# A new order for the same 887 operations of an attention and squared-ReLU kernel, with PSUM rooms shared between its stages

## The chip, the cores and the metric

The kernel runs on one core of one Trainium2 chip. The metric is the device time of one execution in microseconds (us). Three runs of the kernel before took 212.10, 212.76 and 213.73 us; the median is 212.76.

## The reference

Attention with a sliding window of 128 keys and four sink keys, then a two-layer network with a squared ReLU; cut to what is computed:

```python
# q, k, v: (4, 8, 768, 64); n_sink 4; window 128; w_in: (512, 2048); w_out: (2048, 512); float32
scores = (q @ k.transpose(0, 1, 3, 2)) / sqrt(64)
rel = pos[:, None] - pos[None, :]
keep = (pos[None, :] < n_sink) | ((rel >= 0) & (rel < window))
a = softmax(where(keep, scores, -1e9))
x = (a @ v).transpose(0, 2, 1, 3).reshape(3072, 512)
g = maximum(x @ w_in, 0) ** 2
out = g @ w_out                                   # (3072, 512) float32
```

## The kernel before, in words

**Tiling.** The four batches b = 0 to 3 are worked through one after another, with their stages overlapped. A batch has 768 tokens, in three strips s = 0, 1, 2 of 256. Attention of a strip runs in groups: score matmuls (L607) into PSUM, an exponential on ScalarE (L628) that writes `expm` in bf16, masks on `expm` (`domask`: on VectorE, L637 and L640, or as an affine select on GpSimd, which has line L215), the products with v (`values`, L676), and a norm on VectorE (L692 and L693) that gives `xn`. The four sink keys go by `sink_scores` (L566). For batches 0 and 1 queries and keys are transposed on TensorE (L500), and the result of a strip by a bridge on TensorE (L725); for batches 2 and 3 both are DMA transposes on SP's queue: qkT (L454) and xT (L707).

**Layer 1** of batches 0 and 1 is a plain product (L757) with a relu on ScalarE or VectorE (L768, L770) and a square. For batches 2 and 3, `layer1_fast` replaces eight block products by seven: it works on two units, strip 0 alone and strips 1 and 2 together, each in parts of `quad`. Here unit (2, strip 0) or (2, s0) is the first unit of batch 2, and (2, s1) the second. A unit first needs sums of halves of xT (`total`, `xs`, L845, on VectorE); its part is seven products into one PSUM room (L887), numbered as in `product(name, ...)` and run in the order 1, 2, 5, 4, 3, 6, 7. Product 1 needs the first sum. After product 1 `first` copies a bank to `t` (L189 or L191), `less` subtracts product 2 and product 5 from it (L928, VectorE), the relu on the room (L943) must come between products 4 and 3 and the products 6 and 7 that go into the same room, and a custom instruction on VectorE (L955) adds `t`, takes the relu and frees the room. Squares (L909 on ScalarE, L911 on VectorE) write `gT_sb`.

**Layer 2** works on units (b, u) of 256 tokens, u = 0, 1, 2. Two units of batch 0 are plain (L976). The others are `layer2_fast`, with seven products named c, d, a, b, c, d, a by the quarter of the output that they go into (L1086, 8 matmuls of 256 columns each); sums s1 to s4 of `gT_sb` (L1044) come before, and copies and additions (L189, L191, L1111, L1127 `last_quarter`, L1134 `middle`, `first_quarter`) after, into one of two rooms of `osb`, which a 512 KB store on SP (L1163) empties. The last unit, (3, 2), stores in parts (L1156, L1172, L1175).

**Order.** No scheduler decides at run time. The operations are recorded into a plan (`op(...)`: engines with costs, what they come after, which rooms they take and which they release) and issued in the order of the string `ORDER`: one word for each of the 887 operations, the number of the operation, then a letter where the engine is chosen (d VectorE, a ScalarE, g GpSimd), then `+k` where one of several PSUM pools is chosen:

```python
            o.engine = names[word[-1]] if word[-1] in names else next(iter(o.engines))
            for s in o.takes:
                if len(s.pools) > 1:
                    s.pool = s.pools[int(chosen.pop(0))]
                s.room = free[s.pool].pop(0)
```

Each engine runs its own operations in this order; waits between engines follow from the data and from rooms taken over. PSUM is four rooms of two banks each, in two pools of two:

```python
    sizes = dict(att=2, den=2, qr=5, qs=6, expm=8, r=3, osb=2, sg=4, u=2)
```

`att` serves attention and `den` the layers, apart from the first group of batch 0, the groups of batch 1 and `quad`, which may choose. Loads of q, k and v are casting DMAs on GpSimd's queue (L367, L376, L396, L408), for batch 0 also on SP.

Of the kernel before, what the change touches and what calls it, by code (L numbers as in the profile page):

```python
# [21 lines left out]
0 7 8 9 1 5 10 11 2 12 13 3 14 15 55d 57+0 16 19 59a 20 17 56d 21 18 61d 63+0 22 58 62d 65a 60d 64 6 67a 83+1 79 66a  # L22
68d 69+1 85 70 71d 103+0 84+0 105 73g 74d 72d 23 75+1 86 76 77d 91+0 78a 24 87+1 93 25 89 88 92+0 80 26 114+1 90 94
95+0 4 96 117 97 106g 99+1 98 104+0 107 100d 101 118g 81+1 102d 113+0 108d 156 115 127 27 28 29 30 31 32 33 34 35 36
37 38 116d 82 109+0 111 39 40 41 119+1 121 157a 158a 110 112 120 122 162 123+1 125 163d 168 169d 126a 124a 171 172a
170a 159 160d 177 128 131 165 173d 161d 132d 178d 166d 164a 130a 129a 133a 144 146 136 138 174 145 137 289 290 148
134 175a 140 135 176a 147d 167d 139d 291 179d 292 293 141d 142 143 149g 42 43 44 45 46 150 151 47 48 49 50 51 52 53
54 365 366 367 368 208g 369 370 371 372 373 294 295 152 154 296 153d 155d 297d 298d 186 187d 180 181a 200+0 204+1
192+0 201 193 205 194a 206d 195a 189 207d 182d 203a 196+0 197 183 198a 190a 191a 188d 199d 202d 274 212+0+0 184d 209
278 279 215 213 237+0+0 210+1 211 238 240 185d 300 301 275 214 302 241d 276 277 303 280 281 282 304 219+0+0 283 222  # L30
220 306a 305 307 230+0+0 309a 233 231 308 311 223 216 221 310 239d 224+0 312 234g 232g 299 385 386 384 383 313 225
314 242+0 217+0 243 218 284 315 316 235+0 236 285 251+0 286a 287a 317d 252d 253d 244+0 246 226+1 228 247d 227d 245a
248+1 229a 399 322 249d 250d 402 400 323d 355 401 256+0+0 259 257 340 254+0 255 341a 258d 358 356 342a 396 260d 334
335a 374 375 376 377 378 379 380 381 395g 388 390 387 288 392 391 318 389 393 394 331 263+0+0 332a 261+1 264 266 319
262 267d 324d 406 333a 407 320a 337 409 265g 382 597 268+0 598 599 600 601 602 603 604 605 606 607 608 609 610 338a
321d 403 269 328 627d 410 270+0 272 404 408 329a 271a 273d 359 325 405 339a 336a 326a 346 347d 357 327a 415 418 419d
330d 352 411 353a 416 412 354d 447 448 343 344a 345a 349 422 423 425 417g 426g 611 451 452 397 363 449 453d 350d 398
450 351a 348a 454 455 457 466 456a 438 458 459 441 439 467 485 486 489 490 487 460 488 461 361 492 431 491a 432 434
615 413 616 622 620 619 493 462 494d 468 463 464a 414 465 621 617 618 420 440g 612 424g 427 496 433g 442g 428 498
421 470 471 443 435g 436 472a 504a 495 362 499 497 500 473 444 437 508 505 469 628 501 475d 474 477 647 429 625 445  # L40
430 446 650 502a 648 624 503 623 626 360 476 478 481 507 479 506 480 364 482 483d 523+0 525a 524 631 527 526 528 634
632 509+0 510 529 511d 512 530 531a 654 538 633 539 513 514 515 655 533 534 657 649g 656g 516 517a 638 613 614 535
635 536d 537 641 519 520 532a 636 658g 651g 521 639 569+0 570 637 571a 629 583+0 630 572 573 585a 640 522a 518a 574
584 587 575 576 586 555+1 642 589 577a 588 643 679 557a 540 556 590 559 591a 592a 578a 558 560 579 580 593 594 581
561 562 595 541+0 542 683 563a 564a 543d 545 544 680 546 565 547 566 548 684 686 644 567 685a 596a 549a 582a 681
550d 689 682 645 484 646 670 551 552 687 690 673 671 674g 553 688a 554a 663 691 694 666 664 665g 568d 698 692 693
699 659 652 702 703 705 667g 672g 695 696d 700 653 717 660 718 721 668 697 661 736a 704a 669 737 675 676 701 722 739
740 738 708 677 678 662 755+1 706 709 741+1 742 757a 719 720 756 743a 723a 707d 759 745 724 758 761 725 744 760 762
763a 764a 711 746 727 710 713 726a 765 766 747 712 769 714 771 767 728 730 715d 772 748 749a 729 815+0 816 817a 732
770 731 818 733 819 751 752 787+1 734a 735 716 801+0 802 803a 789a 753 820 804 768d 821 788 822 773+1 805 791 754a  # L50
823a 824a 775a 790 806 750d 792 829 807 774 793 776 825 808 794 826 809a 827 830 831 795a 796a 810a 777 779 811 778
812 797 798 833 780 834 836 813 799 828a 835a 781a 832 838d 839 783 784 782a 800a 814a 837 840 841 844 785 786d 842
848 849 852 853 855 843 845 846d 867 854a 850 851 858 857d 868 871 847 856 859 873a 861 862 860 863 864 869 872 865a
866 870 877 874 876a 875 878 880 881 886 879 882 883 885 884
# [59 lines left out]
def kernel(  # L114
# [267 lines left out]

    def load_natural(b, s, older_values):

        P.group = ("load", b)
        begun = [ops["layer1", b - 2, 0, 0], w_out_op[3]]
        for ti in (1, 0):
            if s == 0:
                qn_slot[b, ti] = Slot("qr", NT)
            for i in range(2):  # L390
                t = 2 * s + i

                def run(e, t=t, ti=ti):
                    if t == 0:
                        qn_t[b, ti] = bank(qn_slot[b, ti], "qn", [128, NT, DM], BF16)
                    return [nc.gpsimd.dma_start(  # L396
                        out=qn_t[b, ti][:, t, :].rearrange("p (h d) -> p h d", d=D),
                        in_=(q, k)[ti][b, :, 128 * t:128 * t + 128, :].rearrange("h p d -> p h d"))]
                o = dma_op("pool", ("qk", b, ti, t), run, 64 * 0.032,
                           None,  # L400
                           [qn_slot[b, ti]] if t == 0 else ())
                o.after += begun
                if b - 1 in FAST:
                    o.after += [ops["wi", 1, 0]]
                o.margin = 1.661
        for t in (2 * s, 2 * s + 1):
            def run(e, t=t):
                return [nc.gpsimd.dma_start(  # L408
                    out=v_sb[b % 2][:, t, :, 0:D],
                    in_=v[b, :, 128 * t:128 * t + 128, :].rearrange("h p d -> p h d"))]  # L410
            o = dma_op("pool", ("v", b, t), run, 64 * 0.032)
            o.after += begun + older_values
            o.margin = 1.661
# [6 lines left out]
    def attention(b, key):  # L420
# [3 lines left out]
        begun = [ops["layer1", b - 1, 0, 0]] if b >= 2 and b not in NATURAL else []  # L424
# [12 lines left out]
        def stage(g, f0, f1, side):  # L437
# [4 lines left out]
            def at(f):  # L442
                return key(f0 + (f1 - f0) * f)
# [94 lines left out]
            if g == 0:  # L538
                def sink_keys(e):
                    for h2 in range(2):  # L540
                        r = slice(64 * h2, 64 * h2 + 64)
                        nc.vector.tensor_copy(
                            out=kb[r, :].rearrange("p (m c) -> p m c", c=136)[:, :, 4 * h2:4 * h2 + NSINK],
                            in_=qkT_sb[r, :, 1, 0, 0:NSINK])
# [11 lines left out]
                A["sink_keys"] = op(at(0.1), {"dve": 0.34}, sink_keys,  # L556
# [189 lines left out]
    def layer1(b, key, fbs, c0, cw, need):  # L746
# [3 lines left out]
        bs, rs = Slot("den", 1), Slot("r", 1)  # L750
# [10 lines left out]
        ops["layer1", b, fbs[0], c0] = a  # L761

# [97 lines left out]
    def quad(b, ss, qd, key, xs, sums, slots, part, landed, whole):  # L860
# [15 lines left out]
        def product(name, bk, n, fresh, after):  # L876
# [19 lines left out]
            ops["layer1", b, (f0, name), ss[0]] = o  # L896
            return o
# [19 lines left out]
        m1 = product(1, 0, 0, True, [o for x, o in ops.items() if x[0] == "layer1" and x[1] == b - 1])  # L917
# [43 lines left out]
    def layer2(b, u, keys, by_part=False):  # L961
        P.group = ("l2", b, u)
        bs = Slot("den", 2)
# [57 lines left out]
    def layer2_fast(b, u, key):  # L1021
# [33 lines left out]
        bs, os_, us = Slot("den", 1 if tail else 2), Slot("osb", 1), Slot("u", 1)  # L1055
        ys = Slot("att", 1) if tail else bs
# [84 lines left out]
        pairs = out[128 * g:128 * g + 256, :].rearrange("(i p) m -> p i m" if b in FAST and u else "(p i) m -> p i m", i=2)  # L1141
# [23 lines left out]
        def store_rest(e):  # L1165
            o = bank_t["osb", b, u]
            if b not in FAST or not u:
# [15 lines left out]
    NATURAL, TURNED, BIASED, FAST = (2, 3), (), 1, (2, 3)  # L1183
# [24 lines left out]
    for b in range(B):  # L1208
        if b == 0:
# [3 lines left out]
            at(1, 0.2, 0.725, "att")  # L1213
# [4 lines left out]
        elif b in FAST:  # L1218
            layer1_fast(b, (0,), lambda i, b=b: b + 0.167 * i / 2, 0.01)
            layer1_fast(b, (1, 2), lambda i, b=b: b + 0.167 + 0.34 * i / 4, 0.01)  # L1220
        else:
            for i, fb in enumerate(range(0, NFB, 2)):
                layer1(b, b + 0.34 * i / 8, (fb, fb + 1), 0, 512, (0, 1))
        for i, fb in enumerate(range(0, NFB, 4) if b not in FAST else ()):
            if b == 0:
                layer1(b, 0.2 + 0.226 * i / 4, range(fb, fb + 4), 512, 256, (2,))
            else:
                layer1(b, b + 0.34 + 0.167 * i / 4, range(fb, fb + 4), 512, 256, (2,))
        if b + 1 == FAST[0]:
            weight_sums_in(b + 0.4, [ops[x] for x in ops if x[0] == "layer1" and x[1] == b])  # L1230
        if b + 1 < B:
# [7 lines left out]
            else:  # L1239
                attention(b + 1, lambda f, b=b: b + LO + (HI - LO) * f)(0, 0.0, 1.0, "att")  # L1240
        if b == 0:
            weight_sums(0.6, [w_out_op[i] for i in range(4)])
        for u in range(NS):
            if b == 0 and u < 2:
# [40 lines left out]
```

## Time and profile before

| | |
|---|---|
| median of three runs | 212.76 us (212.10 to 213.73) |
| span of the profiled execution | 210.2 us |
| median less span | 2.56 us |
| TensorE busy | 201.4 us, 96% |
| TensorE weight loads, beside the matmuls | 169.4 us, 81% |
| VectorE busy | 170.8 us, 81% |
| ScalarE busy | 126.6 us, 60% |
| GpSimd busy, its DMA issues included | 101.8 us, 48% |
| granted TensorE clock | 0.99 to 1.00 |
| end of the last matmul | 206.7 us of 210.2 |

The profile is one execution, and the list of times doesn't say which of the three runs it belongs to; its own time is its span and some 2 to 3.5 us that lie around it. In the profile PE is TensorE, DVE VectorE, ACT ScalarE, POOL GpSimd and SP the queue of SyncE; L943 is line 943 of the kernel. A line of a group or of the timeline names the operation, the tile written and the tiles read. What stands behind an arrow in a line of waits is what ended the wait.

### The profile page before, as it was taken

How to read it: one execution, taken by the hardware profiler on the slowest of the kernel's cores; microseconds unless marked ns; L12 is line 12 of the kernel's file. 1: busy time of each engine (PE TensorE's matmuls, PEld its weight loads, DVE VectorE, ACT ScalarE, POOL GpSimd, SP SyncE). 2: the span in 40 equal slices, each digit the busy share in tenths (PEclk: the TensorE clock that was granted, in tenths of full speed). 3: DMA queues.
4: the chain of work that ended last, by engine and by line, in shares of the span. 5: the costliest groups of instructions: out<-in, count | busy, mean ns of one | idle time of the engine just before them, and what ended most of it. 6: DMA issues, size and time to landing. Idle time of an engine off the chain costs nothing.

```text
span 210.2 us, 5719 instructions
## 1 busy us (share of the span) xinstructions
PE 201.4 (96%) x2383; PEld 169.4 (81%) x2383; DVE 170.8 (81%) x317; ACT 126.6 (60%) x162; POOL 101.8 (48%) x143
## 2 busy tenths in 40 slices
PE   3999999999999999999999999799999999999993
PEld 3859996689468845679789988699899999999892
DVE  7487567366999964789997988999989978999863
ACT  2498287407744579898952268889870244896110
POOL 7999774898877941999369023700253000000000
PEclk9999999999999999999999999999999999999998
DMA  5999999999999999999987639700512300400222
GB/s 171 278 188 206 171 201 214 161 155 205 153 112 157 104 150 252 138 124 144 149 102 151 103 77 179 50 3 0 150 62 69 75 5 38 166 0 0 103 100 100
DMA packets 93881, 26.09 MB, mean 124 GB/s; under 512 B 86816, under 2 KB 91552, under 8 KB 93856
## 3 DMA queue, kind: packets, MB, share of 16 engines
q0 software_dynamic: 69248, 12.59, 81.3%
q1 hardware_dynamic: 24424, 13.07, 27.9%
q8 instruction: 18, 0.29, 0.6%
q10 hardware_dynamic: 184, 0.07, 0.1%
q14 instruction: 7, 0.06, 0.1%
HBM read 27.30 MB, written 6.29 MB: 160 GB/s over the span
## 4 chain that ended last, share of the span: by engine, by line
PE 94%; DVE 2%; ACT 1%; POOL 1%; issue 1%; POOLq 0%; DVEq 0%
PE py L1086 29%; PE pm L757 20%; PE pm L887 17%; PE po L676 7%; PE py L976 7%; PE ps L607 6%; PE pt L500 3%; PE pt L182 2%; PE px L725 1%; ACT expm L628 1%; PE ya L1086 1%; PE ps L600 1%; PE pk L566 1%; DVE r L955 1%; DVE gT_sb L911 0%
## 5 line engine op out<-in xcount | busy, mean ns | idle before, releaser
L215 POOL TENSOR_SCALAR_AFFINE_SELECT expm<-expm 128x512 bf16<-128x512 bf16 x42 | 29.2, 724 | 49.5 <-ACT expm L628 24.5
L628 ACT ACTIVATE expm<-ps 128x1024 bf16<-128x1024 f32 (+1 forms) x48 | 43.8, 950 | 12.4 <-PE ps L607 11.3
L757 PE MATMUL pm<-xT,w_in_sb 128*128 128x256 bf16 (+1 forms) x320 | 44.7, 294 | 0.0
L757 PEld LDWEIGHTS <-w_in_sb 128*128 128x128 bf16 x320 | 34.2, 114 | 6.6 <-issue 0.9
L1086 PEld LDWEIGHTS <-gT_sb 128*128 128x128 bf16 x336 | 31.1, 98 | 4.2 <-issue 0.5
L1086 PEld LDWEIGHTS <-sg 128*128 128x128 bf16 x240 | 22.8, 98 | 3.3 <-issue 0.5
L768 ACT ACTIVATE r<-pm 128x1024 bf16<-128x1024 f32 x14 | 14.3, 1022 | 13.5 <-PE pm L757 13.4
L887 PEld LDWEIGHTS <-w_in_sb 128*128 128x128 bf16 x256 | 21.8, 114 | 0.5 <-issue 0.2
L887 PE MATMUL pm<-xs,wi 128*128 128x128 bf16 (+1 forms) x192 | 19.5, 246 | 1.5 <-DVE xs L845 0.9
L1086 PE MATMUL py<-wt,gT_sb 128*128 128x256 bf16 x160 | 20.8, 273 | 0.0
L1086 PE MATMUL py<-wt,sg 128*128 128x256 bf16 x160 | 20.6, 273 | 0.0
L909 ACT ACTIVATE gT_sb<-r 128x1024 bf16<-128x1024 bf16 x18 | 18.4, 1051 | 0.3
L1086 PE MATMUL py<-w_out_sb,gT_sb 128*128 128x256 bf16 x144 | 18.5, 273 | 0.0
L189 ACT ACTIVATE osb<-py 128x256 f32<-128x256 f32 (+1 forms) x15 | 6.2, 410 | 20.3 <-DMA out_dram<-osb 6.0
L770 DVE TENSOR_SCALAR r<-pm 128x1024 bf16<-128x1024 f32 x10 | 12.2, 1222 | 7.5 <-PE pm L757 4.3
L887 PEld LDWEIGHTS <-wi 128*128 128x128 bf16 x192 | 16.4, 113 | 2.2 <-issue 2.1
L693 DVE TENSOR_TENSOR xn_sb<-po,rc 128x512 bf16<-128x512 f32 (+1 forms) x28 | 17.2, 615 | 1.0
L676 PEld LDWEIGHTS <-expm 128*128 128x128 bf16 x352 | 16.3, 97 | 1.4 <-issue 0.5
L676 PE MATMUL po<-v,expm 128*128 128x65 bf16 x352 | 17.3, 193 | 0.1
L943 ACT ACTIVATE r<-pm 128x1024 bf16<-128x1024 f32 x12 | 12.1, 1021 | 8.1 <-PE pm L887 7.9
L928 DVE TENSOR_TENSOR t<-t,pm 128x512 f32<-128x512 f32 x24 | 15.9, 680 | 0.9 <-ACT t L189 0.4
L955 DVE CUSTOM_DVE_ANT_1 r<-pm,t 128x1024 bf16<-128x1024 f32 x12 | 14.5, 1220 | 1.6 <-PE pm L887 1.5
(97 smaller groups left out, 381.9 us busy)
## 6 DMA issues: line engine op xcount, KB each, us to landing
out_dram<-osb SPq DMA_DIRECT2D x11, 512.0 KB, 4.5
v<-in_v_dram POOLq DMA_DIRECT2D x24, 128.0 KB, 7.1
qn<-in_k_dram POOLq DMA_DIRECT2D x20, 128.0 KB, 7.1
qn<-in_q_dram POOLq DMA_DIRECT2D x20, 128.0 KB, 6.9
w_in_sb<-in_moe_w_in_dram POOLq DMA_DIRECT2D x4, 512.0 KB, 10.2
w_out_sb<-in_moe_w_out_dram POOLq DMA_DIRECT2D x4, 512.0 KB, 10.4
qr<-in_k_dram SPq DMA_DIRECT2D x4, 256.0 KB, 5.1
qr<-in_q_dram SPq DMA_DIRECT2D x4, 256.0 KB, 4.8
```

What stands on the lines that cost most here:

```text
L215: nc.gpsimd.affine_select(out=e_tile, in_=e_tile, compare_op=ALU.is_ge, fill=fill, base=i - 1, pattern=[[0, n], [1 if i else -1, 128]], ch ...
L628: nc.scalar.activation(out=x[:, :, o:512], in_=bank_t["s", b, s, m][:, :, o:512], func=AF.Exp, scale=scale)
L676: touch(("po", b, s, m0), e, nc.tensor.matmul(pv[:, i, h2, :], lhsT=lhsT, rhs=rhs, start=(n_ == 0), stop=(n_ == len(mms) - 1)), j)
L693: touch(("po", b, s, m0), e, nc.vector.tensor_tensor(out=xn_sb[:, 2 * s:2 * s + 2, 128 * (m0 + j0):128 * (m0 + j0 + nj)].rearrange("p i (j ...
L757: nc.tensor.matmul(pm[:, i, :], lhsT=w_in_sb[:, fb // 4, kb, fb % 4:512:4], rhs=xT[:, c0 // 256:(c0 + cw) // 256, kb, :], start=(kb == 0), ...
L768: nc.scalar.activation(out=o, in_=h, func=AF.Relu)
L887: touch(tag, e, nc.tensor.matmul(y[:, bk, i, :], lhsT=weights(name, f0 + i, a), rhs=rhs[:, a, :], start=fresh and i == 0 and a == 0, stop= ...
L909: nc.scalar.activation(out=d, in_=x, func=AF.Square)
L928: touch(tag, e, nc.vector.tensor_tensor(out=T["t"], in0=T["t"], in1=T["y"][:, bk], op=ALU.subtract), bk)
L955: touch(tag, e, nc.vector._custom_dve(TENSOR_ADD_SAT, out=r.rearrange("p b n c -> p b (n c)"), in0=T["y"].rearrange("p b n c -> p b (n c)" ...
L976: touch((b, u), e, nc.tensor.matmul(pm[:, i, :], lhsT=gT_sb[:, fb, 128 * t:128 * t + 128], rhs=w_out_sb[:, fb, :], start=(fb == 0), stop=( ...
L1086: ins = nc.tensor.matmul(y_, lhsT=x[:, i, :], rhs=r_, start=(first or tail and n == 2) and i == 0, stop=i == HB - 1, skip_group_check=not ...
```

## The change

The set of operations stays as it is. What changes is

- the string `ORDER`, from about the 24th operation of TensorE on (18.6 us in the trace of before). 267 operations stand on VectorE in place of 274, 170 on ScalarE in place of 161, 100 on GpSimd in place of 102; TensorE keeps 290 and SP 60. Two of the layer-1 relu, the copies of sink keys and some copies go from VectorE to ScalarE, two squares of `quad` the other way; four masks go from GpSimd to VectorE and three back;
- the pools: layer 1, layer 2 and attention may take rooms of `att` and of `den` alike, as the words say;
- bounds on the order that the recorder set: the first product of a `quad` no longer comes after all of the older batch's layer 1, attention no longer after its first product, and the loads of batches 2 and 3 come after whichever layer-1 product was recorded first;
- the copy of sink keys may run on ScalarE;
- `FAST` becomes a table of units, with the same units in it, and the weight sums are recorded later, which shifts numbers in `ORDER`. The tests `b in FAST` turn into `natural` with the same outcome.

In the order of TensorE the stretch from the last product of layer-2 unit (1, 1) to the first product of unit (2, 0) reads, in its first part (numbers are `quad` products; "8" and "12" matmul score groups are `ps`):

```
before: a(1,1) | 1 2 ps 5 | 1' 2' 4 3 ps 5' 4' 6 7 3' ps | 6' 7' values(3,0) | 1 of (2,s1)
after:  1 d(1,1) a(1,1) 2 ps 5 4 1' values(3,0) 2' 3 5' ps 4' 6 3' sinks(3,0) 7 | 1 of (2,s1) | 6' 7' | 2 of (2,s1)
```

(a dash marks the second part of unit (2, s0)). Of VectorE's operations, two sums `xs` of unit (2, s1), the second of them the one that its product 1 needs, stand directly behind `first_quarter` of unit (1, 1); in before that sum is the third of three, and four `less`, a `first`, two masks, a custom relu and a square stand, beside the other two sums, between `first_quarter` and it.

The code, cut to its core:

```diff
 ORDER = """
-0 7 8 9 1 5 10 11 2 12 13 3 14 15 55d 57+0 16 19 59a 20 17 56d 21 18 61d 63+0 22 58 62d 65a 60d 64 6 67a 83+1 79 66a
...
+0 7 8 9 1 5 10 11 2 12 3 55d 13 57+0 14 56d 15 19 20 16 21 61d 59a 17 22 63+0 18 6 62d 58 79 65a 64 60d 67a 68d 83+1
...
 """
+    first_layer1 = {}
...
-        begun = [ops["layer1", b - 2, 0, 0], w_out_op[3]]
+        begun = [first_layer1[b - 2], w_out_op[3]]
...
-        begun = [ops["layer1", b - 1, 0, 0]] if b >= 2 and b not in NATURAL else []
+        begun = []
...
-                A["sink_keys"] = op(at(0.1), {"dve": 0.34}, sink_keys,
+                A["sink_keys"] = op(at(0.1), {"dve": 0.34, "act": 0.42}, sink_keys,
...
-        bs, rs = Slot("den", 1), Slot("r", 1)
+        bs, rs = Slot(("den", "att"), 1), Slot("r", 1)
...
-        m1 = product(1, 0, 0, True, [o for x, o in ops.items() if x[0] == "layer1" and x[1] == b - 1])
+        m1 = product(1, 0, 0, True, [])
...
-        bs = Slot("den", 2)
+        bs = Slot(("den", "att"), 2)
...
-        bs, os_, us = Slot("den", 1 if tail else 2), Slot("osb", 1), Slot("u", 1)
-        ys = Slot("att", 1) if tail else bs
+        bs, os_, us = Slot(("den", "att"), 1 if tail else 2), Slot("osb", 1), Slot("u", 1)
+        ys = Slot(("att", "den"), 1) if tail else bs
...
-    NATURAL, TURNED, BIASED, FAST = (2, 3), (), 1, (2, 3)
+    NATURAL, TURNED, BIASED = (2, 3), (), 1
+    FAST = {2: ((0,), (1, 2)), 3: ((0,), (1, 2))}
...
-            at(1, 0.2, 0.725, "att")
+            at(1, 0.2, 0.725, ("att", "den"))
...
-                attention(b + 1, lambda f, b=b: b + LO + (HI - LO) * f)(0, 0.0, 1.0, "att")
+                attention(b + 1, lambda f, b=b: b + LO + (HI - LO) * f)(0, 0.0, 1.0, ("att", "den"))
```

## The prediction

> **What bounds the kernel now.** I read the page's busy line and slices first, then the waits of TensorE, then the windows, the chain of waits, and last the timeline of the one place where TensorE stands still.
>
> The page:
>
> ```profile
> PE 201.4 (96%) x2383; PEld 169.4 (81%) x2383; DVE 170.8 (81%) x317; ACT 126.6 (60%) x162; POOL 101.8 (48%) x143
> PE   3999999999999999999999999799999999999993
> DVE  7487567366999964789997988999989978999863
> ```
>
> TensorE works 201.4 of the span's 210.2 us; only the first, the last and one slice in the middle fall below 9. The order in which 290 TensorE operations stand cannot shorten the work in them, so all that a new order of the same operations can win is the time in which TensorE stands. The waits of TensorE:
>
> ```profile
> PE pt L182 <- POOL ident L239: 3.5, 1, 3.5
> PE pm L887 <- DVE xs L845: 0.9, 1, 0.9
> PE pm L887 <- ACT r L943: 0.7, 1, 0.7
> ```
>
> The first is the start: nothing to multiply yet. The other two stand together in the one thin slice. The windows of 10 us around it (columns: stretch, length, busy TensorE, weight loads, VectorE, ScalarE, GpSimd, clock, DMA share, GB/s):
>
> ```profile
> 120.00:130.00 10.00, 10.00 (x153) 8.81 (x152) 8.68 (x19) 6.70 (x9) 1.60 (x3) 1.00 0.77 133
> 130.00:140.00 10.00, 8.46 (x109) 7.60 (x107) 9.78 (x15) 9.01 (x12) 5.49 (x8) 1.00 0.49 41
> 140.00:150.00 10.00, 10.00 (x100) 9.31 (x98) 9.76 (x16) 8.71 (x10) 0.00 (x0) 1.00 0.09 23
> ```
>
> From 130 to 150 VectorE is busy 9.8 of each 10 us: here, and nowhere else for long, it and not TensorE sets the pace. The clock is full. The chain of waits through this place (start, length, what):
>
> ```profile
> 128.13 1.92 PE pm L887 x32
> ...
> 130.18 1.22 DVE r L955
> 131.41 0.61 DVE expm L637
> 132.02 1.04 DVE gT_sb L911
> 133.06 0.78 DVE xs L845
> 133.84 0.04 issue
> 133.88 1.03 PE pm L887 x8
> ```
>
> For 3.65 us the end of the kernel hangs on four VectorE instructions in a row. The last, the sum xs for unit (batch 2, strips 1 and 2), is what TensorE needs; the three ahead of it are nothing to it. Now the timeline of the same place (start, length, engine, line):
>
> ```profile
> 130.53 1.02 ACT L943 ACTIVATE r<-pm 128x1024 bf16<-128x1024 f32 x1
> 131.60 1.05 PE L887 MATMUL pm<-xs,wi 128*128 128x128 bf16 x16 [0.68 <-ACT r L943]
> 131.94 1.12 DVE L911 TENSOR_TENSOR gT_sb<-r 128x1024 bf16<-128x1024 bf16 x1
> 132.57 1.75 POOL L215 TENSOR_SCALAR_AFFINE_SELECT expm<-expm 128x512 bf16<-128x512 bf16 x2
> 132.98 0.85 DVE L845 TENSOR_TENSOR xs<-xT 128x512 bf16<-128x512 bf16 x1
> 133.88 0.49 PE L887 MATMUL pm<-xs,wi 128*128 128x256 bf16 x3 [0.86 <-DVE xs L845]
> ```
>
> TensorE stands 0.68 and 0.86 us by the records; counted against its usual rate per matmul (0.109 us for 256 columns, 16 in 1.75) it loses 0.9 and 1.0 there, and 0.1 to 0.2 more at 134.9 and 137.3: some 2.1 us. Before 17 us there are stalls of 0.4 and 0.3 behind the first exponentials (L628), at the end 3.5 us from the last matmul at 206.7 to 210.2. The profiled span is 210.2 and the median run 212.76, so 2.56 us lie around the span (1.9 to 3.5 by the three runs); the sum below is made on the span, and 2.56 added.
>
> **The change part by part.** The operations are the same 887. Up to about 18 us every queue is the same (TensorE's first 24 operations, VectorE's 22, SP's 12), so start and early stalls stay: 0. The last seven products stand in the same order. Store (3,1) is issued some 1.3 us later on SP, behind VectorE's middle sum; the copies into the output room that wait for store (3,0) now have 7 products of 0.87 = 6.1 us of TensorE as cover, against a 512 KB store's median landing of 4.5 us plus 1.1 for the evacuation: 0, and 0.5 to 1 if a landing is late.
>
> Freer PSUM pools (layer1, layer2 and the attention of batches 1 to 3 may use any of the four rooms) issue nothing and remove no work. TensorE in the profile of before waits nowhere for a room that its readers hold longer than about 0.2 us outside 130 to 138, so what they can win elsewhere is 0, and they make the new order possible. The score groups, which cost TensorE 0.12 us each at their end, have as many neighbours of other kinds as before: 0.
>
> Engine moves over the whole kernel: VectorE 274 to 267 operations, ScalarE 161 to 170, GpSimd 102 to 100. Two relu of 1.22 go from VectorE to ScalarE (1.02), copies and sink keys too, two squares of 0.7 come back. VectorE loses some 2 us of 170.8, but outside 120 to 165 it covers nothing that TensorE waits for: 0 there.
>
> Stall one (0.9). Product 6 of unit (2, strip 0) waits for the relu at 130.53, which ran on a ScalarE that had two exponentials ahead; between the product before and it TensorE had one score group (0.44). In the new order there stand sink scores, a product 7 and a product 1: 0.44 + 0.45 + 0.44 = 1.33, which is 0.89 more, as long as the stall. Gone, unless VectorE or ScalarE come later.
>
> Stall two (1.0). The xs sum that product 1 of the next unit waits for is now the second of two right behind the first-quarter copy of unit (1,1), ahead of all that held it back. That wait is gone, but what VectorE did meanwhile stays to be done. So I compare the whole stretch, from the last product of unit (1,1) to the first layer2 product of (2,0). Before: VectorE 30 instructions, 19.2 us busy; it lasted 20.2, TensorE's own work in it is 18.1. After, 32 instructions by the row means: four r at 1.22, twelve t at 0.68, three xs at 0.49 and one at 0.68, two masks at 0.56, two squares and two sg at 0.75, norms 1.8, copies 1.1: 22.2, less the overlap of 0.06 that the timeline shows where one follows another at once, 31 times, is 20.3. TensorE's work in the new stretch is 19.4, as other products have moved in. VectorE therefore still misses TensorE's pace by 0.9, where TensorE lost 2.1 before. Saved: 1.2. Before, the same sum gives 21.2 - 1.7 = 19.5 and 20.2 was needed: 0.5 of idle time ahead of r at 130.18 and hits above the mean. I leave that 0.7 out after, since the sums stand earlier and three of eight GpSimd selects have left the stretch; with it 0.5 is saved. The bounds are 0 (VectorE's total sets the end, whatever stands first) and 2.1.
>
> The contention with GpSimd is in these rows: xs of 128x512 took 0.42 at 127.86 and 0.85 at 132.98 with a select beside it, the square L911 0.69 and 1.12: about 0.43 for a hit. The instructions that read PSUM (r 1.22, t 0.68) take the same time with and without. The five selects left can cost up to 5 x 0.43 = 2.2, of which the row means hold a part already. The Trainium skill (SBUF — State Buffer, "Who interferes with whom") has the rule: a VectorE instruction with two SBUF inputs and a GpSimd one that reads SBUF exclude each other for the whole instruction, whichever began first. By it a hit could cost as long as a select, 0.72, rather than the 0.43 seen, and VectorE would lose up to 5 x 0.72 = 3.6; it also speaks against any order that merely moves the selects. The trace shows nothing above 0.45, and 0.43 is taken.
>
> What is late next. The early xs sums need all of xT, so the last two transposes on SP (L707). On TensorE 7.1 us stand between the second values group of (2,2) and product 2 behind which the sums come, and 1.1 us of VectorE: 8.2. Against it: norm 0.9, three issues on SP of 1.25 (a qkT transpose stands between), the landing 2.5: 7.2. Spare: 1.0. Before, the last issue at 123.58 and 2.5 make 126.1, and the first sum ran at 127.86: 1.8 to spare. The landings on the page of DMAs (median us at the end):
>
> ```profile
> qkT<-qn SPq DMA_TRANSPOSE x24, 5.3
> xT<-xn_sb SPq DMA_TRANSPOSE x12, 2.5
> ```
>
> Of single xT landings the trace has 2.4 to 2.5 near 160 us, 4.1 for the first of these four at 117.4, and 8.1 for one at 97.6. At 4.1 the sums would be 0.6 late. I take back 0.4 for this and for smaller places with little cover (ScalarE's relu and t about 135, its copies behind the middle sum about 154, the norm of values (3,2) about 160); the bounds are 0 and 4.6 (8.1 in place of 2.5, less the spare).
>
> The sum: 210.2 - 1.2 + 0.4 = 209.4; with 2.56 it is 212.0 us.
>
> **The rivals.** *All stalls go.* VectorE's 20.3 would have to be 19.4, two contention hits fewer than I count. For it: eight selects become five. Against it: VectorE at 9.8 of 10 for 20 us, where a wait taken away comes back at the next instruction. 212.76 - 2.1 = 210.6.
>
> *It does nothing that counts.* VectorE's queue is the bound from 126 to 165 and the sums are only done earlier, the relu and t later. For it: the chain hangs on VectorE, whose total in the stretch is no smaller. 212.8.
>
> *Slower: the transposes come late.* The xs sums stand in VectorE's in-order queue where it is the bound; while they wait for xT, everything behind them (less, relu, masks) waits, and TensorE with it. With landing L the cost over my forecast is L - 3.5, from 3.5 on; from 6.4 the whole is 214.9 and the kernel slower by 1%. For it: transposes behind a 512 KB store landed 4.0 us after issue, one xT took 8.1, and two stores stand near in SP's queue. Against it: the landings of 2.5, and the store behind which these would queue is long issued. With 6.5 us it is 215.0.
>
> **How the numbers follow.** Forecast 212.0, chance 0.45 (own range 211.1 to 213.2); all stalls go 0.18; nothing 0.17; transposes late 0.20. A difference of 1%, 2.1 us, is about what a measurement of this kernel can tell. Faster by over 1% (below 210.6) is most of the first rival and a little of the forecast's low side: 0.18. Slower (above 214.9) is the last rival with a bit of "nothing": 0.21. Within: 0.61. The range for 8 in 10 reaches from the first rival, with 0.3 below it, to 215.2.
>
> **What would show it.** Right: no wait of TensorE for relu L943 at 130 us; the sum L845 some 4 us before its product; a thin slice of about 1 us somewhere between 130 and 140 that VectorE ends; VectorE still at 9.7 of 10 there. Wrong: TensorE standing for an xs that itself waits for a transpose (the slower rival); TensorE's busy time up, not its waits (then the rate has changed); waits on L189 or L943 of over 0.5 us away from 130 to 140 (rooms held by late readers, which I put at nothing); or the end, last matmul to last store, longer than 3.5.

## The result: slower by 1.7%, and the profile after

The changed kernel takes 216.5 us (median of 4 runs, 215.75 to 217.02); the kernel before took 212.69 beside it. The ratio is 1.0173, with a 95% interval of 1.0146 to 1.0200. I had forecast 212.0 and a range up to 215.2. Ratios are made of fast executions; that leaves out three of the nine of one run below, the old order with late loads, which took 219.75 to 220.19 us at granted clocks of 0.981 to 0.989.

The page of the changed kernel, the lines that answer to those of before (its lines of code have numbers one to four higher):

```profile
PE 202.3 (94%) x2378; PEld 169.7 (79%) x2383; DVE 167.7 (78%) x310; ACT 130.6 (61%) x174; POOL 94.9 (44%) x137
PE   3989999999999999999949699999999999999993
DVE  7577763499857994999685776999999979988943
```

TensorE's work is what it was, 202.3 against 201.4 us. The thin slice at 130 us is gone, and there are two new ones, the 4 and the 6, at 108 to 113 and 118 to 124 us (a slice is 5.4 us). VectorE is busy 5 to 8 tenths there, so its work isn't what fills this place. The waits of TensorE:

```profile
PE pt L183 <- POOL ident L240: 3.5, 1, 3.5
PE po L678 <- POOL expm L216: 2.9, 2, 2.5
PE py L1090 <- DVE osb L1115: 2.2, 1, 2.2
```

Both waits of before (xs L845, relu L943) have left the list. In their place TensorE waits 2.9 us for masks that GpSimd makes, and 2.2 us for a sum on VectorE. By TensorE's rate per matmul, as in the prediction, the two places lose 3.2 and 2.3 us, where before lost 2.1 at 130 to 138. The first layer-1 product of this execution also came 0.96 us later than in the profile of before (17.79 against 16.83), with the same queues up to there. That isn't the order's: with the old order in the changed program this product starts at 17.6 (the first experiment), and in the profiles of all runs below between 17.1 and 18.2; it is the profile of before that starts early. So 3.2 + 2.3 - 2.1 + 0.96 = 4.4 of the 5.1 us between the two spans (215.3 and 210.2) have a place; the other 0.7 I haven't assigned. The medians lie 3.8 apart. The spans differ by more, since in every run that lists both a time and a span the time is 1.6 to 1.9 us longer: the profile of before is thus an execution of about 211.9 us, 0.8 under the median, and that of after, at 217.02, the slowest of its four.

Why GpSimd is late stands in its own queue (timeline of GpSimd; at the end of a line the idle time before it and what ended that):

```profile
68.29 2.58 POOL L216 TENSOR_SCALAR_AFFINE_SELECT expm<-expm 128x512 bf16<-128x512 bf16 x4 [2.01 <-ACT expm L630]
70.82 1.77 POOL L399 DMA_DIRECT2D qn<-in_q_dram  x2
...
88.28 1.77 POOL L399 DMA_DIRECT2D qn<-in_k_dram  x2
97.39 1.76 POOL L399 DMA_DIRECT2D qn<-in_q_dram  x2 [7.34 <-DMA qkT<-qn]
...
108.95 0.88 POOL L399 DMA_DIRECT2D qn<-in_q_dram  x1
109.84 2.39 POOL L216 TENSOR_SCALAR_AFFINE_SELECT expm<-expm 128x512 bf16<-128x512 bf16 x4
```

Read from the end: the masks at 109.84, for which TensorE waits, stand behind fifteen loads of batch 3. These are late, since the first load of q waited 7.34 us for a buffer, until a qkT transpose of batch 2 had landed. That transpose was late (issued on SP at 88.72, landed at 96.75), since eight loads of q, k and v for batch 2 began only at 70.82; and they stand behind two masks of (1,1), operations 232 and 234, that had waited for exponentials until 68.29.

The order of before has the same two masks on GpSimd, ahead of these loads as well. There they could start at 64.60, since their two exponentials ran from 63.5 to 65.4 rather than from 67.2 to 69.1. The rows of before (their idle time, too, ends with the first exponential, though the row names no releaser):

```profile
64.60 2.85 POOL L215 TENSOR_SCALAR_AFFINE_SELECT expm<-expm 128x512 bf16<-128x512 bf16 x4 [2.66 <-issue]
67.41 0.90 POOL L396 DMA_DIRECT2D qn<-in_q_dram  x1
```

So before, the loads behind these masks began at 67.41 (at 68.58 in the first experiment, the old order with a start nearly as late as here), and the first fourteen loads of batch 3 ran from 85.45 to 98.0 with one idle time of 0.28 us. The other two masks of the strip (1,1) have moved from VectorE to GpSimd, but they are done at 66.28, 2 us before the first of these two can start.

SP's queue carries the lateness on to the second wait:

```profile
99.37 1.19 SPq L709 DMA_TRANSPOSE xT<-xn_sb  x1
100.74 11.22 SPq L457 DMA_TRANSPOSE qkT<-qn  x2
112.01 1.26 SPq L709 DMA_TRANSPOSE xT<-xn_sb  x1
```

Between the two transposes xT of unit (2, s0) stand two of qkT for batch 3, and they take 11.22 us, because the second waits for a q load that lands at 110.3. xT lands at 118.7, and the rest follows in order on ScalarE, VectorE and TensorE:

```profile
118.75 1.06 ACT L190 ACTIVATE xd<-xT 128x1024 bf16<-128x1024 bf16 x1 [3.98 <-DMA xT<-xn_sb]
119.84 0.83 DVE L848 TENSOR_TENSOR xs<-xd 128x512 bf16<-128x512 bf16 x3 [3.90 <-ACT xd L190]
121.06 1.03 PE L1090 MATMUL py<-wt,gT_sb 128*128 128x256 bf16 x8 [2.15 <-DVE osb L1115]
```

TensorE doesn't need xT at 118.6. It needs a sum of layer 2 (L1115) that stands on VectorE behind the sums xs, and these need xT.

### The profile page after: what moved, and what is told of

It reads as the page before. It is cut to its first block, busy times and chain, and to the rows that moved or that the text cites. A ratio compares the mean times of both kernels' runs of the same rounds, so it can differ in the third digit from the quotient of the medians.

```text
span 215.3 us, 5708 instructions
## 1 busy us (share of the span) xinstructions
PE 202.3 (94%) x2378; PEld 169.7 (79%) x2383; DVE 167.7 (78%) x310; ACT 130.6 (61%) x174; POOL 94.9 (44%) x137
## 4 chain that ended last, share of the span: by engine, by line
PE 66%; DMA 17%; SPq 5%; POOL 5%; ACT 2%; issue 2%; DVE 1%; POOLq 0%; DVEq 0%; ACTq 0%
PE py L1090 21%; PE pm L890 18%; PE pm L759 10%; PE py L980 6%; PE po L678 4%; DMA qkT<-qn 4%; DMA qn<-in_q_dram 4%; DMA qn<-in_k_dram 4%; DMA qr<-in_q_dram 3%; PE ps L609 3%; DMA xT<-xn_sb 3%; SPq L457 3%; POOL qn L399 2%; SPq L347 2%; ACT expm L630 2%
## 5 line engine op out<-in xcount | busy, mean ns | idle before, releaser
L216 POOL TENSOR_SCALAR_AFFINE_SELECT expm<-expm 128x512 bf16<-128x512 bf16 x40 | 25.1, 661 | 51.7 <-ACT expm L630 38.4
L678 PE MATMUL po<-v,expm 128*128 128x65 bf16 x352 | 17.9, 193 | 3.0 <-POOL expm L216 2.9
L771 ACT ACTIVATE r<-pm 128x1024 bf16<-128x1024 f32 x16 | 16.2, 1019 | 6.7 <-PE pm L759 6.5
L947 ACT ACTIVATE r<-pm 128x1024 bf16<-128x1024 f32 x12 | 12.3, 1022 | 12.4 <-PE pm L890 11.7
L780 ACT ACTIVATE gT_sb<-r 128x1024 bf16<-128x1024 bf16 x13 | 13.6, 1055 | 5.9 <-DVE r L773 5.7
L913 ACT ACTIVATE gT_sb<-r 128x1024 bf16<-128x1024 bf16 x16 | 16.6, 1054 | 0.4 <-DVE r L959 0.2
L932 DVE TENSOR_TENSOR t<-t,pm 128x512 f32<-128x512 f32 x24 | 15.9, 680 | 0.9 <-PE pm L890 0.2
L190 ACT ACTIVATE osb<-py 128x256 f32<-128x256 f32 (+1 forms) x14 | 5.7, 412 | 16.7 <-PE py L1090 7.5
```

The source lines that it names most:

```text
L216: nc.gpsimd.affine_select(out=e_tile, in_=e_tile, compare_op=ALU.is_ge, fill=fill, base=i - 1, pattern=[[0, n], [1 if i else -1, 128]], ch ...
L678: touch(("po", b, s, m0), e, nc.tensor.matmul(pv[:, i, h2, :], lhsT=lhsT, rhs=rhs, start=(n_ == 0), stop=(n_ == len(mms) - 1)), j)
L771: nc.scalar.activation(out=o, in_=h, func=AF.Relu)
L780: nc.scalar.activation(out=g, in_=r, func=AF.Square)
L913: nc.scalar.activation(out=d, in_=x, func=AF.Square)
L932: touch(tag, e, nc.vector.tensor_tensor(out=T["t"], in0=T["t"], in1=T["y"][:, bk], op=ALU.subtract), bk)
```

## The experiments

In the diffs, words are numbers of operations in the order of the changed kernel; what they are is said ahead of each.

**The old order in the changed program.** All words of the order before, translated to the new numbers, with its engines and PSUM pools.

```diff
-0 7 8 9 1 5 10 11 2 12 3 55d 13 57+0 14 56d 15 19 20 16 21 61d 59a 17 22 63+0 18 6 62d 58 79 65a 64 60d 67a 68d 83+1
+0 7 8 9 1 5 10 11 2 12 13 3 14 15 55d 57+0 16 19 59a 20 17 56d 21 18 61d 63+0 22 58 62d 65a 60d 64 6 67a 83+1 79 66a
...
```

> The changed program with the order, the engines and the PSUM pools of the kernel before: only the freer bounds of the recorder stay. Theory (the order alone lost the time, in the queues of SP and GpSimd): the time of before, 212.7 us. Rival (the looser bounds or the later weight sums change waits of their own): up to 216.5.

Measured: 212.8 us against 212.68, ratio 1.0005 (0.9978 to 1.0032). The looser bounds of the recorder cost and win nothing; the loss is in the order, with the engines and rooms that it names.

**The masks of (2,1) ahead of three loads** (416 and 414 are the masks, 609 to 611 the loads).

```diff
-608 609 610 611 ... 415 446a ... 416g ... 413 414g 429
+608 ... 415 446a ... 416g ... 413 414g 609 610 611 429
```

> The changed kernel; on GpSimd three loads of batch 3 (two k, one q) go behind the two masks of (2,1), which stood behind them; nothing else. Theory: TensorE's wait for the masks at 109 us (2.9 us by the waits) goes, but the later one at 118.6 (2.2 us, for an xT that lands at 118.7 whatever TensorE does) takes up the same time, since it hangs on a clock set by the loads and not on TensorE: 216.5 us, at most 0.5 less, with the second wait grown to about 5. Rival (two waits that add up): 216.5 - 2.9 = 213.6.

Measured: 220.18 us, ratio 1.0343 (1.0301 to 1.0386). The wait for the masks fell from 2.9 to 1.8 us only (GpSimd got its buffer at 98.19 in place of 97.39), and the next one, for L1115, rose from 2.2 to 2.6. So a part of the 1.1 us came back at the second place; the theory had all of it coming back, the rival none. Neither had a loss, and 3.7 us were lost against the changed kernel. That is something else: after each of the two places TensorE's clock is halved, from 112.2 to 115.6 us and from 122.4 to 125.8 (such lines are shown at the end). The mean clock over the span is 0.984 in each of its four runs, 0.016 x 217.6 = 3.5 us of TensorE's time; in the profile of the changed kernel it is 1.000. At the same matmuls, and with the start of the two profiles made equal, TensorE comes out 2.7 us behind the changed kernel, two halvings of 1.7 less a gain of 0.6.

**xT ahead on SP's queue** (403 and 404 are the two xT of (2, s0), 615 and 621 the qkT between them).

```diff
-403 615 628a 621 404 616
+403 404 615 628a 621 616
```

> The changed kernel; on SP's queue the second xT transpose of (2,0) goes right behind the first, ahead of two qkT transposes of batch 3; nothing else. Theory: the second of those qkT transposes waited until 110.4 us for a load of q that landed then, and held xT; without it xT lands by 109, TensorE's wait at 118.6 goes: 216.5 - 2.2 = 214.3 us; the wait for the masks at 109 stays at 2.9. Rival (xT is late by slow DMA queues, landing 6.7 us, not by its place): still over 1 us of wait, above 215.5.

Measured: 218.04 us, ratio 1.0238 (1.0190 to 1.0286), not the 214.3 expected. The wait at 118.6 is gone, so xT was late by its place. But the wait for the masks was 5.2 us in place of 2.9. GpSimd got its buffer at 98.34 rather than 97.39 and waited 0.5 us more for another load, and TensorE came 0.6 earlier. Whether the edit or chance made that transpose land later, one profile doesn't tell. After this wait the clock halves too; three of the four runs have a mean clock of 0.992 and take 218.0 to 218.6, the fourth has 1.000 and takes 216.75.

**Two masks of (1,1) from GpSimd to VectorE**: the start of the chain.

```diff
-228 232g 234g 235+1
+228 232d 234d 235+1
```

> The changed kernel; two masks of (1,1) go from GpSimd to VectorE at the same place of the order; on GpSimd they stood, waiting for exponentials until 68.3 us, ahead of the loads of batch 2. Theory (one root): those loads start 4 us earlier, as in the kernel before, the last qkT transposes of batch 2 too, the q buffers come free and the loads of batch 3 don't wait 7.3 us on GpSimd: both waits of TensorE shrink or go, 211.0 to 212.5 us. Rival (the two late waits have causes of their own at 97 to 110 us, in DMA landings of 7 to 8 us): 215 to 216.5.

Measured: 214.30 us, ratio 1.0077 (1.0055 to 1.0100): 2.2 us better than the changed kernel. The time lies between the two ranges, 1.8 above the theory's and 0.7 below the rival's; the trace decides. The loads of batch 2 began at 66.33, q of batch 3 was loaded at 91.75 without a wait, and both waits of TensorE at 108 to 121 us are gone, as the theory had it; at the end of that stretch TensorE is 3.8 us ahead of the changed kernel. Two new waits took part of it back: 1.3 us at 71.6 for these masks, which stood too late on VectorE, and 1.0 at 133.7 for a qkT transpose of batch 3 behind a store.

**The same, with both new waits mended**: the masks ahead of the middle sum on VectorE, the transpose (625) ahead of the 512 KB store (493) on SP.

```diff
-225 312 315 316 317d 226+0 228 232g 234g 235+1
+225 232d 234d 312 315 316 317d 226+0 228 235+1
...
-624 493 625
+624 625 493
```

> The run with two masks of (1,1) on VectorE, with these masks two steps earlier in VectorE's order (ahead of the middle sum and a copy of layer 2), and one qkT transpose of batch 3 ahead of a 512 KB store on SP. In that run TensorE waited 1.3 us for the masks at 71.6 us and 1.0 us for a qkT transpose at 133.6. Theory: both go, 214.3 - 2.3 = 212.0 us. Rival (the middle sum, 1.3 us later, holds a PSUM room that TensorE needs): no gain at 72 us, 213.3.

Measured: 212.03 us, ratio to the kernel before 0.9975 (0.9960 to 0.9991): what was expected, and the only version whose whole interval lies below the kernel before, by a quarter of a per cent. TensorE's list of waits holds the start and 0.5 us at a bridge (L727), in two pieces.

Moving two masks and one transpose thus takes back the whole loss of the new order, with its engines and rooms otherwise as they are.

**q loads behind k and v loads on GpSimd**, so that GpSimd doesn't stand while q waits for its buffer.

```diff
-598 599 600 601 602 603 604 605 606 607 608 609 610 611
+598 601 602 603 604 607 608 609 610 599 600 605 606 611
```

> The changed kernel; on GpSimd five loads of q for batch 3 go behind the eight loads of k and v that followed them, so that the k and v loads run while q waits for its buffer (the buffer comes free at about 97 us, when the last qkT transpose of batch 2 has landed). Theory: GpSimd is through its loads at 102 us and not at 110, the masks of (2,1) are made in time (2.9 us of TensorE's waits go), and the q load behind which SP holds xT lands 3 us earlier, so the second wait keeps about the 2.2 us or a little more: 213.3 us, range 212.5 to 214.5. Rival (the masks are late by their exponentials or by VectorE, not by the loads ahead on GpSimd): 216.

Measured: 217.84 us, ratio 1.0249 (1.0204 to 1.0294). GpSimd was through its loads at 104 us, the masks came in time, and the first wait is gone, as expected. But the q load behind which SP stands landed at about 110 as before, though its issue was 1.2 us earlier. So xT was issued at 111.38 (112.01 in the changed kernel), TensorE, now 3.2 us ahead, waited 3.3 for it, until 119.4. From 118.3, still in this wait, the clock was halved for 6.8 us (a mean clock of 0.984 in the profiled execution; the four have 0.984 to 0.996).

**The same with xT ahead on SP's queue.**

```diff
-403 615 628a 621 404 616
+403 404 615 628a 621 616
```

> The kernel before this one in the list (q loads behind k and v loads), and the second xT transpose of (2,0) ahead of the two qkT transposes on SP's queue. Theory: both waits of TensorE between 108 and 121 us are gone, 5.3 us together with nothing in their place: 211.2 us, the first version under the old order's 212.7; between 120 and 140 us TensorE waits at most 1 us. Rival (once the waits at 110 to 120 us are gone, VectorE's backlog shows between 125 and 140, as I forecast it): 212.1 with a wait of about 0.9 for VectorE there.

Measured: 216.44 us, ratio 1.0178 (1.0137 to 1.0220), where 211.2 was expected. (Two of the four executions have a mean clock of 0.992; the profiled one, of 216.48 us, has 0.998.) At 121 us TensorE was 5.5 us ahead of the changed kernel, so both waits were indeed gone. Then the next ones came, none of them VectorE's backlog that the rival named:

```profile
PE py L1090 <- ACT osb L190: 2.5, 1, 2.5
PE pm L890 <- DVE t L932: 1.1, 1, 1.1
PE pk L568 <- ACT r L947: 1.1, 1, 1.1
```

SP's queue shows where the first of them is from:

```profile
101.96 16.36 SPq L457 DMA_TRANSPOSE qkT<-qn  x6
118.42 0.53 SPq L1168 DMA_DIRECT2D out_dram<-osb  x1
```

Six qkT transposes of batch 3 wait on SP for their loads until 118.4, and a store stands behind them. ScalarE's copy into `osb` waits for the room that this store empties. My theory had the two waits right and the cure wrong: as long as the loads are late, whatever stands behind them on SP is the next to wait.

**q loads first on GpSimd.**

```diff
-371 372 597 598 599 600 601
+599 600 371 372 597 598 601
```

> The changed kernel; on GpSimd the first two q loads of batch 3, which wait for the last qkT transpose of batch 2 to land, go ahead of the two v and two k loads that stood before them. Theory (the transpose, issued at 88.7 us, takes 8 us to land because those four loads were issued into the DMA queues just ahead of it): it lands some 3 us after its issue, GpSimd goes on at about 92 us and not at 97.4, all later loads follow 1.5 to 2 us earlier (four loads of 0.9 now stand behind): the masks are made by 110.5, the wait of 2.9 us shrinks by 1.5 to 2; 214.5 to 215.5 us. Rival (the landing is long by itself, or by loads issued long before): GpSimd waits until 97 as before with four loads more to issue, both waits grow by 3.5: 219 or more.

Measured: 216.86 us, ratio 1.0201 (1.0142 to 1.0260); the one run with a full clock took 215.62. Neither sequence came out as expected. The q loads didn't wait at all. The buffers for q and k come from one pool of five, dealt out in the order of issue: q now got the free one, and k waited 4.7 us, until 95.25. A load of q (87.04) and a store of 512 KB (87.22) were still issued just ahead of the transpose in question, and three more loads right behind it; it took 6.8 us from 87.85. So this run doesn't tell why it lands so late.

**The old order with late loads**: one v load (371) and the sink values of batch 2 (385) ahead of seven loads of batch 2, which are 2.8 us later by that.

```diff
-364 365 366 367 368 369 370 371 385g
+385g 371 364 365 366 367 368 369 370
```

> The old order; on GpSimd one v load (0.9 us) and the sink values of batch 2 (1.9 us), neither needed soon, go ahead of the last seven loads of batch 2, so that these are 2.8 us later; nothing else. Theory (the loss hangs on how late these loads are): the last qkT transposes of batch 2 are issued 2 to 3 us later, land behind newly issued loads, the q loads of batch 3 wait on GpSimd for their buffer, and masks or xT come late for TensorE: 214 to 217 us with waits of TensorE between 98 and 122 that the old order doesn't have. Rival (the old order has more than 3 us of slack there, and the new order lost its time elsewhere): 212.7.

Measured: ratio 1.0060 (1.0024 to 1.0097), from six executions of 213.57 to 215.57 us beside a kernel before of 212.88: a loss, near the lower end of the theory's range. GpSimd shows the wait of the changed kernel, and TensorE a new one beside the two of before:

```profile
93.81 1.75 POOL L399 DMA_DIRECT2D qn<-in_q_dram  x2 [5.44 <-DMA qkT<-qn]
```

```profile
PE py L1090 <- DVE sg L1048: 1.8, 1, 1.8
```

So the old order too has no slack for 2.8 us there: a small delay of the loads at 70 us comes back as a wait of 5.4 on GpSimd at 93, and as 2.0 us lost on TensorE at 107.

**The old order with one sum early**: the xs sum for which TensorE waited 0.9 us in the kernel before (537), four operations earlier on VectorE (a `less`, a custom relu, a mask and a square).

```diff
-539 ... 514 ... 535 635 536d 537
+539 537 ... 514 ... 535 635 536d
```

> The old order, with one sum xs on VectorE ahead of a less, a relu, a mask and a square: the sum for which TensorE waits 0.9 to 1.0 us at 133 us in the kernel before. Theory of my forecast (VectorE's total sets the end of the stretch): the wait goes but comes back behind the relu and the less that are 0.4 later, at most 0.5 us gained: 212.2 to 212.7. Rival (the wait alone costs, since the work behind it has slack): 1.0 gained, 211.7.

Measured: 212.18 us, ratio 0.9993 (0.9978 to 1.0007): no difference that can be told, and within what the theory allowed. In the trace the wait for xs is gone, 0.2 us behind `t` L932 is new, and TensorE gains 0.5 over the stretch.

## Why the prediction was wrong

**The step that failed** is the 0 for what lies outside 120 to 165 us: the moved work "covers nothing that TensorE waits for: 0 there". I priced the new order there by the busy time of the engines and by TensorE's waits before, followed SP's queue only from about 115 us on, and looked at GpSimd only for its collisions with VectorE. But a new order can make waits that the old one doesn't have. In the new one the scores of strip (1,1) come later, so two masks on GpSimd wait for their exponentials until 68.3 us, and the loads of batch 2 behind them begin at 70.8. In the trace of before GpSimd, too, stands ahead of these masks (2.66 us), but TensorE waits for nothing of it, so TensorE's waits of before couldn't show it. What the runs showed in place of the 0: 5.5 us of new waits at 108 to 121, all of them gone with these two masks moved to VectorE. That the new order began the loads too late was tried from the other side as well: the old order with seven of these loads 2.8 us later loses 0.6%. The move of the strip's two other masks to GpSimd has no run of its own.

**The slower rival** had the right kind of thing, a transpose late on SP with VectorE's in-order queue behind it, but the wrong one. I took the last two xT, of unit (2, s1), with a landing as the unknown, and gave it a spare of 1.0 us. TensorE never waited for those, so that the direction came out is no hit for the mechanism. The one that was late was the second xT of unit (2, s0), not by its landing but by a qkT transpose ahead of it on SP that waited for its load. I named "a qkT transpose stands between" for the other pair and counted 1.25 us of issue for it; what counts is what that transpose itself waits for.

**What is late next** was to be asked of the loads, too: the 512 KB stores, the masks and the transposes of batch 3 stand behind them in two queues, and the runs with q last, and with xT ahead as well, met them one after another.

**Stall one and stall two** went as forecast: neither is in the list after. The stretch between unit (1,1) and unit (2,0) came out better than my 20.3 us of VectorE. It lasted 19.30 with TensorE busy throughout and VectorE 18.67 (columns as in the prediction):

```profile
131.46:150.76 19.30, 19.30 (x273) 18.42 (x271) 18.67 (x31) 16.51 (x22) 3.86 (x7) 1.00 0.32 84
```

My 22.2 us of rows were 20.5: ten `t` and the start of an eleventh, not twelve, and xs at 0.42 and squares at 0.68 where I took means that hold collisions with GpSimd. The overlap was the 0.06 for each instruction that I took. So the whole 2.1 of stalls was saved there, not 1.2; the rival "all stalls go" was right on this stretch, and the thin slice between 130 and 140 that I gave as a sign of being right didn't come. The mended order shows the same 19.30. It gains only 0.5 us over the kernel before: some 0.9 it gives back in small waits at 71 to 74 us, around the masks, and 0.7 I haven't assigned.

**The 2.56 us** that I added to the span are not what lies around a span: the runs have 1.6 to 1.9 there, and the rest is that the profiled execution was faster than the median. It moves the forecast by less than 1 us and isn't the step that failed.

**Stalls shift when VectorE is the bound**: that part of the argument held where it was tried alone, in one profile. With one sum earlier in the old order, the wait of 1.0 us became a gain of 0.5 on TensorE; the time of the runs can't tell it from nothing.

**The pools.** Looser bounds with the old rooms do nothing: 1.0005. The new choice of rooms has no run of its own; the mended order keeps it and loses nothing, so no run speaks against the 0 that I put for it.

**Left open**: why a qkT transpose lands 8 us after its issue in the changed kernel (88.72 to 96.75). Three loads of 128 KB were issued in the 2.2 us ahead of it, a fourth 0.4 us behind it, and a store of 512 KB 0.7 us ahead of it on the same queue. Before, q was loaded at 87.19 without a wait, so the last transpose of its buffer, issued at 83.94, had landed within 3.3 us. I didn't find a run that takes the loads or the store away and leaves the rest. Why the first layer-1 product starts anywhere from 16.8 to 18.2 us is open as well.

## What to carry to other kernels

Where engines run fixed orders, follow each queue for what its instructions wait for, DMA queues first, and over the whole span: a mask that waits on GpSimd delays every load behind it, and that can surface 40 us later on TensorE. An order that has been shortened by use of slack must be checked at the buffers that link the queues; here five q and k buffers did it. To mend such a chain, work at its head: the edits further down moved the wait on, and the one at the head took it away.

## What the hardware showed that I had not expected

**A pause can halve TensorE's clock for a while.** After the 4.8 us pause of the run with xT ahead, the clock goes to a half, then back (windows of 1 us; the clock is the third number from the end):

```profile
113.00:114.00 1.00, 0.26 (x3) 0.15 (x4) 0.00 (x0) 0.00 (x0) 1.00 (x3) 0.94 2.73 151
114.00:115.00 1.00, 1.00 (x20) 1.00 (x21) 0.00 (x0) 0.00 (x0) 0.99 (x2) 0.50 2.63 151
...
116.00:117.00 1.00, 1.00 (x7) 0.71 (x5) 0.96 (x2) 0.00 (x0) 1.00 (x2) 0.50 1.53 121
117.00:118.00 1.00, 1.00 (x10) 0.82 (x9) 0.69 (x1) 0.83 (x4) 0.69 (x1) 0.85 1.56 127
```

Some 3.4 us at half speed, or 1.7 us lost, on top of the pause. In the run with the masks ahead a pause of 2.6 us was enough, and so were two of 1.0 and 0.8 us with one matmul between them. Pauses of 2.5 and 2.2 us (the changed kernel), 2.5 (q last and xT ahead) and 2.7 (q first) left the clock at 1.00 in the profiled executions, so its length alone doesn't say whether a pause does it. The Trainium skill (TensorE: Matmul & The Clock Gate, "What's actually happening") has a window of about 3.4 us that runs freely, after which an idle array is throttled and a busy one released. The length of the slow phase agrees (3.4 us three times, and 6.8 in the run with q last); pauses shorter than the window tripped it here.

**GpSimd's masks can hold a VectorE instruction for far longer than the 0.43 us that I took for a collision.** In the changed kernel one addition of 128x256, 0.42 us with no mask beside it, took 2.87 while four masks ran back to back from 109.84 to 112.2:

```profile
110.10 2.87 DVE L1131 TENSOR_TENSOR osb<-osb,u 128x256 f32<-128x256 f32 x1
```

The prediction set the rule of the Trainium skill (SBUF — State Buffer, "Who interferes with whom"), by which the one that comes second waits, against 0.45 us as the most that the trace showed. This row fits the rule, and the addition waited for all four and not only for the mask that was running: it ended at 112.97, 0.7 us after the last of them, of which 0.42 is its own time and 0.3 isn't explained. In the run with the masks ahead a mask on VectorE took 2.32 us from 107.96, in place of 0.68: it waited for three masks of GpSimd, and the fourth then took 1.10 in place of 0.64.
